# The last product of a packed-attention and gated-feed-forward kernel as one level of Strassen's seven products from batch 2 on

## The chip, the cores and the metric

The kernel runs on one core of one Trainium2 chip. A core has TensorE (in profiles PE for its matmuls and PEld for its weight loads), VectorE (DVE), ScalarE (ACT), GpSimd (POOL), and SyncE (SP), whose queue issues nearly all DMA transfers here. The metric is the device time of one execution in microseconds, the median of several runs.

## The reference

All inputs are float32. There are 8 batches, 8 heads, 576 tokens and a head width of 64; 32 packed queries stand for each head. The output has 4608 rows (8 × 576 tokens) of 512 columns.

```python
def sm_attn(qq, kk, vv):
    s = scale * np.matmul(qq, kk.transpose(0, 1, 3, 2))
    s = s - np.max(s, axis=-1, keepdims=True)
    a = np.exp(s)
    a = a / (np.sum(a, axis=-1, keepdims=True) + 1e-09)
    return np.matmul(a, vv)
p_packed = sm_attn(p, k, v)
x = sm_attn(q, p_packed, p_packed)      # then (B*S, 512)
h = x @ w_in                            # 512 -> 2048
g = h * (1.0 / (1.0 + np.exp(-1.702 * h)))
out = g @ w_out                         # 2048 -> 512
```

## The kernel before

**Two parts.** For each batch the attention makes a small matrix `a` (the softmax weights of the 576 tokens over 32 packed rows of 8 heads, 256 rows in all) and four chunks of a matrix `m` (the packed values times `w_in`, 256 × 2048). The feed-forward part then forms `h = m^T a`, passes it through the gate, and multiplies the result `g` by `w_out`. The matmuls of the feed-forward part work on float32 split in two: an upper part, rounded to the fp32r type (`mhi`, `ahi`, `ghi`, and part 0 of `wo`), and the rest, rounded likewise (`mlo`, `alo`, `glo`, part 1 of `wo`). A product of two such numbers is three matmuls: upper × upper, upper × lower, lower × upper.

**First product.** `h_mm` (L693 to L701) makes 128 of the 2048 hidden columns for one half of a batch, 288 tokens, in one bank of PSUM: 2 × 3 = 6 matmuls of 128 × 288 (L698). Two banks (`psh`) take turns.

**Gate.** ACT writes a tanh of `h` (`h_tanh`, L706), DVE multiplies it with `h` (`h_gate`, `h_over`, L688), ACT or DVE rounds the result to `ghi` (`h_upper`, L121 or L123), and DVE or POOL writes the rest to `glo` (`h_lower`, L685).

**Last product.** `out_mm` (L758, in `product`) adds, for one block of 128 hidden columns `f` and one block of 128 tokens `i`, three matmuls with the tokens' `g` as the stationary operand and 512 columns of `w_out` as the moving one to one of four PSUM banks `acc0` to `acc3`. A batch has four whole token blocks, so each `f` takes 12 matmuls of 512 columns. The last 64 tokens of each batch (`REST`) are put aside in SBUF (`over`), and two batches together make one more block of 128 tokens (`over_mm`). Over the whole kernel L758 stands for 1728 matmuls of 512 columns. After the last `f`, `out_take` copies a bank to SBUF and `store` writes 256 KB to the output.

**Attention of the next batch.** It runs among the feed-forward work of the current one. On PE it comes as blocks of small matmuls that use parts of the array: `scores1_mm` (L265), `pack` (L459), `scores2_mm` (L588) and `m_chunk` (L528, 8 matmuls for each quarter of `w_in`), and one small transposition (`pack_turn_mm`, L518). A float32 matmul that is not fp32r stands in the profile as two records. `w_in` stays in SBUF for the whole run. The loads of `k`, `v` and `q` of a batch have tiles from a pool with two buffers (`kqv`), so that `q` may be loaded while `v` is still being read.

**What sets the order.** A tuple `order` lists some 2,900 steps, and a loop at the end of the function calls them one after another; each engine runs its share in that order, and each DMA queue too. Semaphores between engines follow from the tiles that steps read and write.

Of the kernel before, what the change touches and what calls it, by code (L numbers as in the profile page):

```python
# [18 lines left out]


@with_exitstack
def kernel(
    ctx: ExitStack,
    tc: tile.TileContext,
    q: bass.AP,
# [7 lines left out]
):  # L33

    nc = tc.nc

    NFC, NP, P, FC = w_in.shape
    DM, DF = NP * P, NFC * FC
    D = P // 2
    B = q.shape[1]  # L60
    NH = q.shape[3] // NP
    S = 2 * NH
    KF = 2 * P
    NPK = pk.shape[2] // NP - KF
    G = S // NPK
    NF = DF // P
    CF = FC // P
    NB = S // P
    REST = S - NB * P
    KC = (S + P - 1) // P  # L70
    KLAST = S - (KC - 1) * P
    DEC = 3
    MB = 2
    LATE = [(B - 1, 2), (B - 1, 3)]
    SCALE = 1.0 / float(D) ** 0.5

    cst = ctx.enter_context(tc.tile_pool(name="cst", bufs=1))
    wk = ctx.enter_context(tc.tile_pool(name="wk", bufs=1))
    ps_acc = ctx.enter_context(tc.tile_pool(name="ps_acc", bufs=1, space=PSUM))
    ps_h = ctx.enter_context(tc.tile_pool(name="ps_h", bufs=2, space=PSUM))  # L80
    ps_b = ctx.enter_context(tc.tile_pool(name="ps_b", bufs=2, space=PSUM))

    ident = cst.tile([P, P], F32, name="ident")
    make_identity(nc, ident)

    minus = cst.tile([P, P], F32R, name="minus")
    nc.scalar.mul(minus, ident, -1.0)

    w_in_all = cst.tile([P, NFC, NP, FC], F32, name="w_in")
    w_in_sb = [w_in_all[:, i] for i in range(NFC)]  # L90
    w_in_end = w_in_all.rearrange("p c j f -> p (c j f)")[:, NFC * NP * FC - NP * S :]
    w_in_raw = w_in.bitcast(U16)
    w_out_raw = w_out.bitcast(U16)

# [21 lines left out]
    def bank_acc(i):
        return lambda name: ps_acc.tile([P, FC], F32, tag=f"acc{i}", name=name)
# [19 lines left out]


    def load(what, b, part):
        if (what, b) not in kq:  # L140

            if what == "q" and b == 0:
                t = w_in_end
            else:
                t = wk.tile([P, KC * DM], F32, tag="kqv", name=f"{what}_{b}", bufs=2)
            kq["t", what, b] = t
            if what == "k":
                kq["p", b] = t[:, : NP * NPK].rearrange("p (j n) -> p j n", n=NPK)
            if what == "v":
                kq[what, b] = t.rearrange("p (c e) -> p c e", e=DM)  # L150
            else:
                at = NP * NPK if what == "k" else 0
                t = t[:, at : at + NP * S]
                n = KF if what == "k" else NH
                kq[what, b] = [
                    i.rearrange("p (j s) -> p j s", j=NP) for i in (t[:, : NP * n], t[:, NP * n :])
                ]
        t = kq["t", what, b]
        if what == "v":
            main = (KC - 1) * DM  # L160
# [20 lines left out]
    raw = {}  # L181
    wo = {}
# [3 lines left out]


# [3 lines left out]
    def load_w(n, part=None):  # L191
        w = queue[n]
        i = slot_of(w)
# [4 lines left out]
        if not part:  # L198
            raw[i] = wk.tile([P, DM, 2], U32, tag=f"wo{i}", name=f"raw{i}")
        halves = raw[i].rearrange("p n w -> p (n w)").bitcast(U16)  # L200
# [3 lines left out]

    tops = wk.tile([P, 4, DM], U32, tag="late", name="tops")
    tops = [tops[:, i, :] for i in range(4)]
    for t in tops:
        nc.gpsimd.memset(t, 0)
    dec = {}
    top = {}

    def begin_w(n, part=None):
        top[n, part] = tops[(n + (part or 0)) % 4]  # L220
# [32 lines left out]

    def lower_w_copy(n, engine=nc.scalar):
        move(engine, wo[slot_of(queue[n])][:, 1, :], st["wl", n])

# [1301 lines left out]
```

## Time and profile before

| | us |
|---|---|
| median of 3 runs (691.46 to 691.87) | 691.49 |
| span of the profiled execution | 689.5 |
| PE busy (5020 matmul records) | 680.5 |
| DVE busy | 411.3 |
| ACT busy | 256.1 |
| POOL busy | 159.8 |

The span runs from the first to the last instruction of one profiled execution; the time of a run lies some 2 us above it. Matmuls are pipelined, and the recorded length of one is longer than the distance to the next; what a matmul costs is read from the starts of matmuls that follow each other without a wait.

### The profile page before, as it was taken

The numbers are of one execution on the slowest core, as the hardware profiler recorded it, in microseconds if no ns is written. First come the engines' busy times: TensorE is split into PE (matmuls) and PEld (weight loads), VectorE is DVE, ScalarE is ACT, GpSimd is POOL, SyncE is SP. The second block draws the span as 40 slices with busy tenths as digits, with TensorE's granted clock in tenths as the row PEclk, the third lists the DMA queues.
The fourth block names the chain that finished last, engine by engine and source line by source line (L and its number), as shares of the span: only waits on it lengthen the run. The fifth ranks groups of instructions, "written<-read, shape, count | busy, mean of one in ns | idle before, by whom it ended". The sixth has DMA issues, their size and how long they took to land.

```text
span 689.5 us, 13004 instructions
## 1 busy us (share of the span) xinstructions
PE 680.5 (99%) x5020; PEld 559.2 (81%) x5020; DVE 411.3 (60%) x1046; ACT 256.1 (37%) x617; POOL 159.8 (23%) x191
## 2 busy tenths in 40 slices
PE   8899999999999999999999999999999999999997
PEld 6678788888888888888778878888887878878885
DVE  5998877465565665546646458736565457664333
ACT  4886545222242234332324332523244322342220
POOL 2543351112520123221311012120221120310220
PEclk9999999999999999999999999999999999999999
DMA  9998602501135130430313420252301500010002
GB/s 343 397 355 247 252 37 50 177 16 35 62 90 137 39 111 4 104 120 1 92 54 87 138 61 1 82 130 73 115 17 62 130 1 1 16 62 1 1 1 77
DMA packets 55262, 65.20 MB, mean 95 GB/s; under 512 B 35808, under 2 KB 40864, under 8 KB 54176
## 3 DMA queue, kind: packets, MB, share of 16 engines
q1 hardware_dynamic: 55120, 64.23, 28.9%
q8 instruction: 40, 0.66, 0.4%
q14 instruction: 22, 0.18, 0.1%
q10 hardware_dynamic: 80, 0.13, 0.1%
HBM read 50.78 MB, written 13.57 MB: 93 GB/s over the span
## 4 chain that ended last, share of the span: by engine, by line
PE 96%; DVE 1%; ACT 1%; DMA 1%; POOL 0%; issue 0%; SPq 0%; DVEq 0%; ACTq 0%; POOLq 0%
PE acc L758 52%; PE h L698 30%; PE acc_over L758 6%; PE psm_None L528 4%; PE ps L588 1%; PE pspv L459 1%; PE ps L265 1%; DMA k<-k_last 1%; DVE w_in L234 0%; POOL x L623 0%; PE psm L528 0%; ACT tops L222 0%; ACT x L344 0%; PE pspt L518 0%; DVE x L599 0%
## 5 line engine op out<-in xcount | busy, mean ns | idle before, releaser
L758 PE MATMUL acc<-wo,ghi 128*128 128x512 f32 x1024 | 321.2, 395 | 0.0
L758 PEld LDWEIGHTS acc<-wo,ghi 128*128 128x128 f32 x1024 | 181.4, 188 | 34.8 <-issue 5.1
L706 ACT ACTIVATE g<-h 128x288 f32<-128x288 f32 x256 | 103.2, 411 | 273.8 <-PE h L698 246.8
L758 PE MATMUL acc<-wo,glo 128*128 128x512 f32 x512 | 201.6, 394 | 0.0
L685 POOL TENSOR_TENSOR glo<-g,ghi 128x288 fp32r<-128x288 f32 (+1 forms) x136 | 103.0, 765 | 425.2 <-ACT ghi L121 153.7
L688 DVE SCALAR_TENSOR_TENSOR g<-g,h 128x224 f32<-128x224 f32 (+1 forms) x256 | 105.1, 416 | 127.1 <-ACT g L706 126.1
L698 PE MATMUL h<-ahi,mhi 128*128 128x288 f32 x480 | 135.9, 298 | 0.1
L698 PE MATMUL h<-ahi,mlo 128*128 128x288 f32 x480 | 134.5, 295 | 0.3 <-DVE mlo L564 0.3
L758 PEld LDWEIGHTS acc<-wo,glo 128*128 128x128 f32 x512 | 96.1, 188 | 22.6 <-POOL glo L685 0.3
L698 PEld LDWEIGHTS h<-ahi,mhi 128*128 128x128 f32 x480 | 90.2, 188 | 20.0 <-DVE x L599 10.1
L698 PE MATMUL h<-alo,mhi 128*128 128x288 f32 x480 | 101.3, 292 | 0.0
L698 PEld LDWEIGHTS h<-ahi,mlo 128*128 128x128 f32 x480 | 90.4, 188 | 6.2 <-DVE mlo L564 0.5
L698 PEld LDWEIGHTS h<-alo,mhi 128*128 128x128 f32 x480 | 77.1, 188 | 0.1
L121 ACT CAST ghi<-g 128x224 fp32r<-128x224 f32 (+1 forms) x133 | 52.8, 404 | 50.5 <-DVE g L688 29.7
L685 DVE TENSOR_TENSOR glo<-g,ghi 128x288 fp32r<-128x288 f32 (+1 forms) x120 | 53.4, 447 | 20.5 <-ACT ghi L121 17.9
L688 DVE SCALAR_TENSOR_TENSOR over<-g,h 128x64 f32<-128x64 f32 x128 | 26.9, 215 | 36.0 <-ACT g L706 35.8
L123 DVE CAST ghi<-g 128x288 fp32r<-128x288 f32 (+1 forms) x123 | 37.9, 313 | 12.5 <-PE acc L758 9.5
L564 DVE TENSOR_TENSOR mlo<-psm_None,mhi 128x512 fp32r<-128x512 f32 x58 | 38.5, 677 | 2.6 <-ACT mhi L121 2.3
L758 PE MATMUL acc_over<-wo,ghi_over 128*128 128x512 f32 x128 | 39.8, 392 | 0.0
L528 PE MATMUL psm_None<-w_in,PT 64*32 64x512 f32 x496 | 33.0, 595 | 0.0
L758 PEld LDWEIGHTS acc_over<-wo,ghi_over 128*128 128x128 f32 x128 | 23.7, 188 | 4.8
L121 ACT CAST mhi<-psm_None 128x512 fp32r<-128x512 f32 x34 | 19.6, 585 | 21.0 <-PE psm_None L528 21.0
(108 smaller groups left out, 509.1 us busy)
## 6 DMA issues: line engine op xcount, KB each, us to landing
v<-v SPq DMA_DIRECT2D x8, 1024.0 KB, 5.4
o<-o SPq DMA_DIRECT2D x32, 256.0 KB, 3.2
raw<-w_out SPq DMA_DIRECT2D x16, 511.8 KB, 5.7
q<-q SPq DMA_DIRECT2D x14, 576.0 KB, 5.3
raw<-w_in SPq DMA_DIRECT2D x12, 511.8 KB, 7.7
k<-k_last SPq DMA_DIRECT2D x8, 640.0 KB, 4.7
k<-pk SPq DMA_DIRECT2D x8, 576.0 KB, 4.9
aside<-xb SPq DMA_DIRECT2D x56, 72.0 KB, 2.3
```

What stands on the lines that cost most here:

```text
L121: nc.scalar.copy(dst, src)
L123: engine.tensor_copy(dst, src)
L265: nc.tensor.matmul(bank[32 * j : 32 * j + 32, : k.shape[1]], kq["p", b][rows(eo), j, :], k, start=True, stop=True,)
L459: nc.tensor.matmul(bank[32 * j : 32 * j + 32, e * D : (e + 1) * D], aT[:, c, e, 32 * j : 32 * j + 32], vt[:, c, e0 : e0 + D], start=(c == ...
L528: nc.tensor.matmul(banks[eo][32 * j : 32 * j + 32, columns(part)], PT[rows(eo), j, :], w_in_sb[fc][rows(eo), j, columns(part)], start=True ...
L564: nc.vector.tensor_tensor(lo, bank[:, at], hi.bitcast(F32), op=ALU.subtract)
L588: nc.tensor.matmul(banks[eo][32 * j : 32 * j + 32, :NH], st["PT", b][rows(eo), j, :], kq["q", b][half][rows(eo), j, :], start=True, stop=True,
L685: engine.tensor_tensor(lo, src, hi.bitcast(F32), op=ALU.subtract)
L688: nc.vector.scalar_tensor_tensor(dst, th, 1.0, h, op0=ALU.add, op1=ALU.mult)
L698: nc.tensor.matmul(h[:, :NH], m[eo][part][:, fo : fo + P], a[:, eo * NH : (eo + 1) * NH], start=(n == 0), stop=(n == len(terms) - 1),)
L706: nc.scalar.activation(g, st["h", b, f, half][:, :NH], AF.Tanh, scale=1.702)
L758: nc.tensor.matmul(acc, gp[:, at : at + P], wo[f][:, part, :], start=(start and i == 0), stop=(stop and i == 2),)
```

## The change

Batch 0 keeps the last product of before. Everything behind it is rebuilt.

- A batch's tokens are cut into unequal halves of `NA` = 256 and `NB_` = 320. A round `n` is one half of a batch (`n` = 2 to 15, two for each batch from 1 on), or, twice, the 256 tokens that four batches put aside (`("over", 0)` and `("over", 1)`). Of the 320 tokens of an odd round, the first 64 are the ones put aside, now to a DRAM tensor (`over_kept`, by `hp_over`), and read back by `over_in`.
- A round has 8 pairs `p` of hidden blocks. For each pair `hp_mm` makes `h` of both blocks in a double bank `hh` (12 matmuls of 256 or 320 columns), and one tanh and one gate handle both. 
- A pair is then a 2 × 2 block product: two token blocks by two hidden blocks, times two hidden blocks by two column halves of `w_out` of 256. `sums_1` to `sums_3` make four sums of blocks of `g`; `g_upper` and `g_lower` round the seven blocks that are used. `product` does the seven products, each three matmuls of 256 columns, to seven half banks. `take_1` to `take_6` add these up when a round ends.
- The sums of blocks of `w_out` are made once, pair by pair (`conv_whole`, `conv_1` to `conv_4`, `conv_upper`, `conv_lower`) during rounds 2 to 5, and stay in SBUF (`RUNS`). Until a pair's sums are there, the pair is done in the way of before (`plain`): these are the 15 pairs of `PLAIN`; the other 113 of 128 use the seven products.
- Memory is laid out by hand in named regions. `w_in` is written to DRAM after batch 0 (`win_out`) and each quarter of it is read back for each later batch (`win_in`, 1 MB), since its place now holds the rounded `g` and some sums. For batches from 2 on `k`, `v` and `q` share one region, `KQ[0]`. Blocks of `g` before rounding have two places in turn (`g_words`), as have the rounded ones.

```diff
-    def product(acc, g, f, at, start, stop):
-        for i, (part, gp) in enumerate(((0, g[0]), (1, g[0]), (0, g[1]))):
-            nc.tensor.matmul(
-                acc, gp[:, at : at + P], wo[f][:, part, :],
-                start=(start and i == 0), stop=(stop and i == 2),
-            )
+    def hp_mm(n, p, j):
+        h_terms(hh()[:, j, :], n // 2, 2 * p + j, n % 2)
+    def hp_over(n, p):
+        b = n // 2
+        g = hp_view(n, p)[0][:, :, :REST]
+        dst = over_kept[b // 4][p].rearrange("p (j t) b r -> p j t b r", t=2)
+        nc.sync.dma_start(dst[:, :, b % 4 // 2, b % 2, :], g)
+    def over_in(n, p):
+        src = over_kept[n[1]][p].rearrange("p i b r -> p (i b r)")
+        nc.sync.dma_start(g_words(n, p, 0, 4 * P), src)
+    def sums_1(n, p, engine=nc.vector):
+        a, e = g_at(n, 1), g_at(n, 2)
+        src = g_words(n, p, a, 2 * (e - a)).rearrange("p (i t) -> p i t", i=2)[:, :, :P]
+        dst = g_raw(n, p, 4, 2).rearrange("p (i t) -> p i t", i=2)
+        by = g_raw(n, p, 0).unsqueeze(1).broadcast_to([P, 2, P])
+        engine.tensor_tensor(dst, src, by, op=ALU.subtract)
+    def sums_2(n, p, engine=nc.vector):
+        engine.tensor_tensor(g_raw(n, p, 6), g_raw(n, p, 5), g_raw(n, p, 1), op=ALU.add)
+    def sums_3(n, p, engine=nc.vector):
+        engine.tensor_tensor(g_raw(n, p, 7), g_raw(n, p, 3), g_raw(n, p, 6), op=ALU.subtract)
+    PRODUCT = {
+        1: (1, 0, 0), 6: (6, 0, 256), 5: (5, 1, 0), 7: (4, 1, 256), 2: (3, 2, 0), 3: (7, 2, 256),
+        4: (2, 3, 0),
+    }
+    def product(n, p, k):
+        block, i, at = PRODUCT[k]
+        hi, lo = (g_block(n, p, part, block) for part in range(2))
+        bhi, blo = moving(p, k)
+        add_up(n, i, at, 256, [(hi, bhi), (hi, blo), (lo, bhi)])
+    def take_3(n):
+        nc.vector.tensor_tensor(
+            o_words(n, 256, 512).rearrange("p (i t) -> p i t", i=2),
+            acc[1].rearrange("p (i t) -> p i t", i=2),
+            u2().unsqueeze(1).broadcast_to([P, 2, 256]), op=ALU.add,
+        )
+        at = KQ[b < 2 and what == "v"] if (what, b) != ("q", 0) else WIN + NFC * NP * FC - NP * S
...
-        (out_mm, 7, 14, 0), (out_mm, 7, 15, 0), (h_lower, 7, 14, 1), (h_gate, 7, 15, 1),
+        (hp_mm, 15, 1, 0), (g_upper, 15, 0, 0, act), (g_upper, 15, 0, 1, dve),
+        (g_lower, 15, 0, 1, dve), (hp_mm, 15, 1, 1), (g_lower, 15, 0, 0, dve), (product, 14, 7, 1),
```

The order of the instructions moves with it. On PE, in the middle of batch 4 before: `out_mm` (L758, hidden blocks of 128, `wo` and `ghi` or `glo` as operands) between the first products (L698) of single hidden blocks.

```order
L758 MATMUL acc_4_4407<-wo_584,ghi_2_4402 128x512 x2
L758 MATMUL acc_4_4407<-wo_584,glo_2_4403 128x512
L698 MATMUL h_0_5_4553<-ahi_0_4261,mhi_1_0_4416 128x288
L698 MATMUL h_0_5_4553<-ahi_0_4261,mlo_1_0_4417 128x288
L698 MATMUL h_0_5_4553<-ahi_0_4261,mhi_1_1_4355 128x288
L698 MATMUL h_0_5_4553<-ahi_0_4261,mlo_1_1_4356 128x288
L698 MATMUL h_0_5_4553<-alo_0_4262,mhi_1_0_4416 128x288
L698 MATMUL h_0_5_4553<-alo_0_4262,mhi_1_1_4355 128x288
L758 MATMUL acc_4_4442<-wo_584,ghi_2_4402 128x512 x2
L758 MATMUL acc_4_4442<-wo_584,glo_2_4403 128x512
```

And in the changed kernel, where the first half of a batch passes into the second (L698 is `h_terms`, L863 the matmuls of `product`; all rounded operands have names of regions).

```order
L698 MATMUL hh<-at_float32r 128x256 x12
L863 MATMUL acc_63<-at_float32r 128x256 x6
L863 MATMUL acc_64<-at_float32r 128x256 x6
L863 MATMUL acc_65<-at_float32r 128x256 x6
L863 MATMUL acc_66<-at_float32r 128x256 x3
L698 MATMUL hh<-at_float32r 128x320 x12
```

A stage of PE is now 12 matmuls of the first product and 21 matmuls of 256 columns, where two hidden blocks and 256 tokens took 12 of 512 columns.

DVE in the feed-forward work of a batch before (L688 gate and the part put aside, L123 rounding):

```order
L688 SCALAR_TENSOR_TENSOR g_0_12_3075<-g_0_12_3075,h_0_12_3058 128x288
L123 CAST ghi_12_3091<-g_0_12_3075 128x288
L688 SCALAR_TENSOR_TENSOR over_3_3096<-g_1_12_3094,h_1_12_3065 128x64
L688 SCALAR_TENSOR_TENSOR g_1_12_3094<-g_1_12_3094,h_1_12_3065 128x224
L123 CAST ghi_12_3091<-g_1_12_3094 128x224
```

DVE for one pair of an even round in the changed kernel (L691 is the gate, L826 to L834 the sums, L173 rounding, L841 `g_lower`):

```order
L841 TENSOR_TENSOR at_float32r<-at_float_349,at_float32r 128x512
L691 SCALAR_TENSOR_TENSOR at_float_349<-at_float_349,hh 128x512
L826 TENSOR_TENSOR at_float_349<-at_float_349 128x256
L830 TENSOR_TENSOR at_float_349<-at_float_349 128x128
L834 TENSOR_TENSOR at_float_349<-at_float_349 128x128
L173 CAST at_float32r<-at_float_349 128x384
L841 TENSOR_TENSOR at_float32r<-at_float_349,at_float32r 128x384
```

Three sums stand between a gate and the rounding now, and the two roundings of the rest are of 384 (448 in odd rounds) and 512 columns.

SP around the load of `q` in the middle of the run before (L447 brings the turned attention weights `aT` in, L171 loads `k` and `q`): `q` goes to a tile of its own.

```order
L447 DMA aT<-aside_4414 32x4x256 x2
L447 DMA aT<-aside_4414 32x256
L447 DMA aT<-aside_4414 32x4x256
L171 DMA q_4793<-q 128x1152 x2
L171 DMA k_4387<-k_last 128x1280
```

And in the changed kernel (L498 brings `aT` in, L814 is `hp_over`, L917 `keep`, L223 and L225 load `q`), with the semaphores that each waits for:

```order
L498 DMA at_float_92<-aside_2268 32x256 [waits DMAHW7_49]
L498 DMA at_float_92<-aside_2268 32x256
L814 DMA over_94<-at_float_349 256x1x64 [waits DMAHW1_49,DVE_49]
L223 DMA at_float_97<-q 128x1024 [waits DMAHW2_49,PE_49]
L225 DMA at_float_97<-q 128x1280 [waits DMAHW3_49,PE_49]
```

The load of `q` now waits for PE, that is for `pack`, which reads `v` in the same region. On PE, `pack` (L511) and the first use of that `q` (`scores2_mm`, L617) are one stage apart in a later batch of the changed kernel:

```order
L511 MATMUL b_68<-at_float_97,at_float_92 32x64 x4
L863 MATMUL acc_63<-at_float32r 128x256 x6
L562 MATMUL b_67<-at_float_74,at_float_243 128x128
L863 MATMUL acc_64<-at_float32r 128x256 x6
L863 MATMUL acc_65<-at_float32r 128x256 x6
L863 MATMUL acc_66<-at_float32r 128x256 x3
L698 MATMUL hh<-at_float32r 128x320 x6
L617 MATMUL b_67<-at_float_97,at_float_249 32x256
```

The blocks of small matmuls have moved too. Before, 14 of the `m_chunk` blocks follow a `scores2_mm`, 6 stand with both `scores1_mm` of a batch and 6 with a `pack`, with no large matmul between; with the 7 that stand otherwise there are 33 such blocks on PE behind the start. In the changed kernel 30 `m_chunk`, 13 `scores1`, 12 `scores2_mm` and 7 `pack` stand alone and 2 `m_chunk` with a `scores2_mm`: 64 blocks. 

## Rows read from the trace of the kernel before

**Rows 1.** The page's first part: the span, and busy time, share and count by engine, and from its second part the granted TensorE clock in 40 slices, in tenths.

```profile
span 689.5 us, 13004 instructions
PE 680.5 (99%) x5020; PEld 559.2 (81%) x5020; DVE 411.3 (60%) x1046; ACT 256.1 (37%) x617; POOL 159.8 (23%) x191
PEclk9999999999999999999999999999999999999999
```

**Rows 2.** The page's chain of waits that ended last, by engine and by line, as shares of the span.

```profile
PE 96%; DVE 1%; ACT 1%; DMA 1%; POOL 0%; issue 0%; SPq 0%; DVEq 0%; ACTq 0%; POOLq 0%
PE acc L758 52%; PE h L698 30%; PE acc_over L758 6%; PE psm_None L528 4%; PE ps L588 1%; PE pspv L459 1%; PE ps L265 1%; DMA k<-k_last 1%; DVE w_in L234 0%; POOL x L623 0%; PE psm L528 0%; ACT tops L222 0%; ACT x L344 0%; PE pspt L518 0%; DVE x L599 0%
```

**Rows 3.** The chain of waits in order of time: start, length and count of matmuls on it, for two runs of matmuls of 512 columns without another between.

```profile
666.57 7.53 PE acc L758 x33
674.10 11.01 PE acc_over L758 x48
```

**Rows 4.** The timeline of PE, start and length in us: the first matmuls of two neighbouring first products and the first matmul behind them. Twelve matmuls of 288 columns start from the first row to the second.

```profile
300.93 0.29 PE L698 MATMUL h<-ahi,mhi 128*128 128x288 f32 x1
...
302.51 0.63 PE L758 MATMUL acc<-wo,ghi 128*128 128x512 f32 x2
```

**Rows 5.** The timeline of PE and of its weight loads: matmuls of 128 columns with a new load each, back to back at the start.

```profile
14.67 2.72 PE L129 MATMUL warm<-ident 128*128 128x128 f32 x22
...
14.89 2.31 PEld L129 LDWEIGHTS warm<-ident 128*128 128x128 f32 x20
```

**Rows 6.** The timeline of PE around blocks of small matmuls: the block's start, and the start of the next large matmul. In the second stretch the last large matmul ahead, and in the first the second one behind, stand too.

```profile
24.85 0.77 PE L265 MATMUL ps<-k 64*32 64x320 f32 x16
25.55 0.40 PE L698 MATMUL h<-ahi,mhi 128*128 128x288 f32 x1
25.79 0.30 PE L698 MATMUL h<-ahi,mlo 128*128 128x288 f32 x1
...
50.87 0.40 PE L758 MATMUL acc<-wo,glo 128*128 128x512 f32 x1
51.20 1.09 PE L528 MATMUL psm_None<-w_in,PT 64*32 64x512 f32 x16
52.22 0.40 PE L698 MATMUL h<-ahi,mhi 128*128 128x288 f32 x1
...
69.74 1.32 PE L459 MATMUL pspv<-v,aT 128*32 128x64 f32 x80
71.00 0.73 PE L758 MATMUL acc<-wo,ghi 128*128 128x512 f32 x2
...
104.49 1.09 PE L528 MATMUL psm_None<-w_in,PT 64*32 64x512 f32 x16
106.48 0.73 PE L758 MATMUL acc<-wo,ghi 128*128 128x512 f32 x2
...
221.53 1.09 PE L528 MATMUL psm_None<-w_in,PT 64*32 64x512 f32 x16
223.80 0.73 PE L758 MATMUL acc<-wo,ghi 128*128 128x512 f32 x2
...
230.64 0.72 PE L588 MATMUL ps<-q,PT 64*32 64x288 f32 x16
231.15 1.06 PE L528 MATMUL psm_None<-w_in,PT 64*32 64x512 f32 x16
232.14 0.40 PE L698 MATMUL h<-ahi,mhi 128*128 128x288 f32 x1
```

**Rows 7.** Groups of DVE instructions by line and shape: count, busy us, mean ns of one, and idle time before them.

```profile
L688 DVE SCALAR_TENSOR_TENSOR g<-g,h 128x288 f32<-128x288 f32 x128 | 57.4, 450 | 80.9 <-ACT g L706 80.0
L688 DVE SCALAR_TENSOR_TENSOR g<-g,h 128x224 f32<-128x224 f32 x128 | 48.6, 382 | 46.3 <-ACT g L706 46.2
L564 DVE TENSOR_TENSOR mlo<-psm_None,mhi 128x512 fp32r<-128x512 f32 x58 | 38.5, 677 | 2.6 <-ACT mhi L121 2.3
L685 DVE TENSOR_TENSOR glo<-g,ghi 128x288 fp32r<-128x288 f32 x68 | 32.9, 487 | 10.5 <-ACT ghi L121 8.5 <-PE acc L758 0.3
L685 DVE TENSOR_TENSOR glo_over<-over,ghi_over 128x512 fp32r<-128x512 f32 x10 | 8.0, 797 | 3.1 <-ACT ghi_over L121 2.9
```

**Rows 8.** The tanh on ACT, likewise.

```profile
L706 ACT ACTIVATE g<-h 128x288 f32<-128x288 f32 x256 | 103.2, 411 | 273.8 <-PE h L698 246.8 <-POOL glo L685 15.3 <-DVE glo L685 7.8
```

**Rows 9.** DMA issues by kind: count, KB each, median us from issue to landing.

```profile
v<-v SPq DMA_DIRECT2D x8, 1024.0 KB, 5.4
o<-o SPq DMA_DIRECT2D x32, 256.0 KB, 3.2
q<-q SPq DMA_DIRECT2D x14, 576.0 KB, 5.3
aside<-xb SPq DMA_DIRECT2D x56, 72.0 KB, 2.3
aT<-aside SPq DMA_DIRECT2D x28, 128.0 KB, 2.6
```

**Rows 10.** The timeline of SP around one load of `q`, and of PE for that batch's `pack` and `scores2_mm`.

```profile
388.40 2.00 SPq L171 DMA_DIRECT2D q<-q  x2
...
387.02 1.32 PE L459 MATMUL pspv<-v,aT 128*32 128x64 f32 x80
...
399.46 0.72 PE L588 MATMUL ps<-q,PT 64*32 64x288 f32 x16
```

More of the change, by code (lines that the diff above doesn't have):

```diff
@@ L577, in m_again_copy @@
-    def m_again_copy(b, fc, eo, part=None, engine=nc.scalar):
-        at = columns(part)
-        move(engine, st["m", b, fc, eo][1][:, at], st["again", b, fc, eo, part][:, at])
-    def scores2_mm(b, half, banks=(bank_b, bank_b)):
-        st["x", 2, b, half] = x_tile(f"x2_{b}_{half}")
-        banks = [bank(f"ps2_{b}_{half}_{eo}") for eo, bank in enumerate(banks)]
+        hi, lo = (m_part(fc, eo, i)[:, at] for i in range(2))
+        t = st["bank", "m", b, fc, eo, part]
+        nc.vector.tensor_tensor(lo, t[:, at], hi.bitcast(F32), op=ALU.subtract)
@@ new lines, in take_4, with take_5, take_6, keep @@
+    def take_4(n):
+        nc.vector.tensor_tensor(
+            o_words(n, 768, 256), acc[1][:, 256:], o_words(n, 256, 256), op=ALU.add
+        )
+    def take_5(n):
+        o = o_words(n, 0, 512)
+        nc.vector.tensor_tensor(o, acc[2], o, op=ALU.add)
+    def take_6(n):
+        whole = any(not SET[m, p] for m, p in G_INDEX if m == n)
+        o = o_words(n, 512, 512 if whole else 256)
+        nc.vector.tensor_tensor(o, acc[3] if whole else acc[3][:, :256], o, op=ALU.add)
+    def keep(n, i, engine=nc.sync):
+        src = o_words(n, 0 if i else 512, 512)
+        at = n // 2 * S + (NB_ if n % 2 else 0) + i * P
+        engine.dma_start(out[at : at + P, :], src)
@@ new lines @@
+        (plain, 3, 4, 1, 1), (g_upper, 3, 6, 0, act), (sums_2, 3, 6, dve),
+        (conv_upper, 4, -1, dve), (sums_3, 3, 6, dve), (m_chunk, 2, 1, (6, 7), None),
+        (g_lower, 3, 6, 0, dve), (g_upper, 3, 6, 1, act), (hp_mm, 3, 7, 0),
+        (conv_lower, 4, -1, dve), (m_upper, 2, 1, 0, None, act), (win_in, 2, 2),
+        (m_upper, 2, 1, 1, None, dve), (g_lower, 3, 6, 1, pool), (hp_mm, 3, 7, 1),
+        (m_lower, 2, 1, 0), (m_lower, 2, 1, 1), (product, 3, 5, 1), (conv_whole, 3, 1, pool),
@@ new lines @@
+        (g_lower, 7, 5, 1, dve), (hp_tanh, 7, 6), (product, 7, 4, 6), (product, 7, 4, 5),
+        (hp_gate, 7, 6), (product, 7, 4, 7), (product, 7, 4, 2), (hp_over, 7, 6),
+        (sums_1, 7, 6, dve), (product, 7, 4, 3), (product, 7, 4, 4), (sums_2, 7, 6, dve),
+        (sums_3, 7, 6, dve), (m_chunk, 4, 1, (6, 7), None), (g_upper, 7, 6, 0, act),
+        (g_upper, 7, 6, 1, dve), (hp_mm, 7, 7, 0), (g_lower, 7, 6, 1, dve),
+        (m_upper, 4, 1, 1, None, act), (win_in, 4, 2), (g_lower, 7, 6, 0, dve),
@@ new lines @@
+        (product, 11, 4, 2), (hp_over, 11, 6), (sums_1, 11, 6, dve), (product, 11, 4, 3),
+        (product, 11, 4, 4), (sums_2, 11, 6, dve), (sums_3, 11, 6, dve),
+        (m_chunk, 6, 1, (6, 7), None), (g_upper, 11, 6, 0, act), (g_upper, 11, 6, 1, dve),
+        (hp_mm, 11, 7, 0), (g_lower, 11, 6, 1, dve), (m_upper, 6, 1, 0, None, act), (win_in, 6, 2),
+        (g_lower, 11, 6, 0, dve), (m_upper, 6, 1, 1, None, act), (hp_mm, 11, 7, 1),
+        (m_lower, 6, 1, 0), (product, 11, 5, 1), (hp_tanh, 11, 7), (m_lower, 6, 1, 1),
```

2458 lines of the change are left out of this document (1362 added, 1096 removed).

## The prediction

> **What bounds the kernel now.** [...] Then the chain of waits: 96% of it is PE, and 58% of the span is L758, the product that changes [rows 2]. So time follows the work on PE, and the other engines matter where they come near PE's time or are late for it. Recorded lengths of matmuls overlap, so starts are counted. Runs of 33 and of 48 matmuls of 512 columns last 7.53 and 11.01 us, 228 and 229 ns each [rows 3]; the chain's 58% over 1728 matmuls gives 231, and I take that, since it holds all of them [rows 2]. Twelve matmuls of 288 columns last from 300.93 to 302.51, 132 ns each [rows 4].
>
> **What a matmul of 256 columns costs.** None of full array size is in the trace. From the two points the slope is (231 - 132)/224 = 0.442 ns a column: 256 columns give 118 ns and 320 give 146. Below, 111 ns is conceivable (the slope of the fastest starts); above, 132, what 288 columns cost, bounds it, if something other than columns sets the distance. A weight load per matmul is such a thing: 22 matmuls of only 128 columns, each with a load, last 2.72 us, and 20 loads 2.31, about 112 ns apart [rows 5]. That is below 118, so I take 118. [...]
>
> **The product on PE.** Of 1728 matmuls of 512 columns 372 stay (192 in batch 0, 15 plain pairs of 12). The other 1356, 113 pairs of 12, become 113 x 21 = 2373 of 256 columns. Off: 1356 x 231 ns = 313.2 us. On: 2373 x 118 = 280.0. **Gain 33.2 us**, 294 ns a pair. The first product keeps its columns: 768 x (118 + 146) ns is what 1536 x 132 was, so 0.
>
> **Small matmuls on PE now stand alone.** A block costs its time inside and two edges. The row of 512 columns ahead of the block at 51.20 starts 0.33 us earlier in place of 0.23, an edge of 0.10; behind the block at 24.85 the next distance is 0.24 in place of 0.13, 0.11 [rows 6]. With 0.2 for edges a lone `m_chunk` costs 1.02 + 0.2, `scores1` 0.70 + 0.2, `pack` 1.26 + 0.2; with company 1.50 + 0.2 (`scores2_mm`), 2.27 + 0.2 (`pack`) and 1.99 + 0.2 (two `scores1`) [rows 6]. A lone `scores2_mm` is not in the trace behind the start: it is between its 0.51 ahead of `m_chunk` and the 0.70 of `scores1`, plus 0.2; I take 0.8. Before: 14 x 1.70 + 6 x 2.47 + 6 x 2.19 + 7 others of about 9.9 = 61.6 us. After: 30 x 1.22 + 13 x 0.90 + 12 x 0.80 + 2 x 1.70 + 7 x 1.46 = 71.5. **Loss 9.9 us.**
>
> **DVE.** Two-input instructions cost 487 ns for 288 columns and 677 for 512, the gate 382 for 224 and 450 for 288 [rows 7]: about 150 + 1.05 a column. Per pair of an even round DVE has a gate of 512 (688), sums of 256, 128 and 128 (419 + 2 x 284), `g_lower` of 512 and 384 (688 + 553), and one of two roundings (some 0.4): 3.3 us against 12 x 118 + 21 x 118 = 3.9 on PE; in odd rounds the gate is of 640 and one `g_lower` of 448, 3.5 against 12 x 146 + 2478 = 4.2. Over the kernel the counts of the new program times these lengths add up to some 185 us (sums +89, `g_lower` +68, adding up `take_*` +33, block sums of `w_out` +25, fewer and wider gates -35, rounding +5), so DVE rises from 411 to some 595 of 670, 89%. POOL and ACT change by less than 20 us. So PE stays ahead in nearly every stage, but with little room. The gate frees `hh` for the next first product: tanh of 640 (some 0.7, from 411 ns for 288 [rows 8]) and gate (0.82) take 1.6 of the 2.5 us of products that cover them; if DVE starts the gate over 0.9 us late, PE waits. The new waits of DVE upon itself (gate, three sums, rounding, each reading the last one's result) have behind them on DVE the attention's work; who waits is PE's next product, a stage later. I take 0.5 us for all of it, between 0 and rival B.
>
> **Transfers with PE behind them.** (1) `q` now waits for `pack`, in batches 2 to 7. Queued on SP behind it are only `hp_over` and `win_in`. From the end of `pack` to `scores2_mm` PE has 2.48 us of products, a transposition (0.15) and six matmuls of 320 (0.88): 3.5 us. The first half of `q` is 512 KB: between 3.2 us for 256 KB and 5.4 for 1 MB, about 4, plus 0.1 to issue [rows 9]. PE then stands 0.6 us, six times: **3.6 us**; at the 5.3 us of the old `q` 11, at 3.2 none. Before, 11 us lay between that load and its use [rows 10]. (2) The last of six `aT` loads, each some 0.45 us of SP apart, behind `keep` and so behind `take_6`, lands 2.6 us after its issue [rows 9]; `pack` stands one stage (4.2 us) behind the first. 0 to 1 us, six times; I take 0.25, nearer to nothing, since the first of the six may be issued before that stage begins: 1.5. (3) In the `over` rounds no first product covers anything: 256 KB in (3.2), sums and `g_lower` (1.7), then the place is free, some 5.1 us for two pairs against 4.96 on PE. 0 to 6 us for both rounds, I take 2. (4) `win_in` of 1 MB lands in 5.4 [rows 9] and has two stages (8 us) or more: 0, hidden by products; `hp_over` (64 KB, like `aside` with 2.3 us) has two stages until its place is written again: 0. Without that cover each would cost what it lacks. **Together 7.1 us.** Start and end keep their shape: 0.
>
> **Sum.** On the profiled execution 689.5 - 33.2 + 9.9 + 0.5 + 7.1 = 673.8; runs stand 2.0 above the span: **676 us.** The edges were counted in the 231 already to some part (clean runs are 229 [rows 3]); with 229 for the old matmuls and 117 for the new, the gain would be 1356 x 229 - 2373 x 117 = 32.9, so that does not move the sum.
>
> **Rivals.**
> A, PE alone decides: no wait of the last two parts shows, and 256 columns cost their fastest, 114. 691.5 - 33.2 - 2373 x 4 ns (9.5) + 9.9 = 659 (between that and the forecast lies the same mechanism with other sizes). For it: idle PE before is a few us [rows 1, 2]. Against: the two narrow places above.
> B, DVE becomes the bound from batch 2 on. The row of `glo_over` means 797 ns where the same shape from PSUM means 677 [rows 7]: DVE's two-input instructions are held up at times by something. With some 40 ns on 620 such instructions (25 us) and 33 ns for each of some 250 more waits on itself (8), DVE has 628 us, and with what it cannot use at the start and between tanh and gate (some 60) the run takes 688. It decides from about 4.0 us of DVE a stage. [...]
> C, slower: load and matmul do not overlap fully, and 256 columns cost as much as 288, 132 ns. Then 3141 matmuls of 256 (2373 and 768) cost 14 ns more, 44 us: 676 + 44 = 720. It decides from about 123 ns, where the gain is gone (16/3141 = 5 ns above 118). For it: the load's 112 ns is close. Against: twelve matmuls of 288 keep 132, which is 20 above the load's distance, without a sign of a floor.
> D, the seven products are not what runs: the counts of the new program (2373 of 256 columns) exclude it.
>
> **How the numbers follow.** Forecast (663 to 684) 0.70; A 0.12; B 0.10, about a third of it no better than now; C 0.08. Range 655 to 692: it leaves out C and a little of A. A measurement of this kernel tells 0.2% (1.4 us) from no change. Faster: 0.70 + 0.12 + 0.06 = 0.88; within 0.2%: 0.02; slower: 0.02 + 0.08 = 0.10.
>
> **What would show it.** In the new profile, starts of L863 in a row 118 ns apart (C: over 123); PE busy 97% or more (B: DVE near its whole span, and PE's idle time ended by DVE); idle time ahead of `scores2_mm` ended by the DMA of `q`, about 0.6 us six times; ahead of `pack` by `aT`; in the `over` rounds by DVE or DMA; blocks at 1.2 and 0.9 us. Wrong would be 118 in the first place: each ns of it is worth 3.1 us.

## The result and the profile after

The changed kernel takes 697.19 us (median of 4 runs, 696.11 to 697.79) where the kernel before takes 691.48 (691.25 to 691.87): a ratio of 1.0079, 95% interval 1.0065 to 1.0093. It is 5.7 us slower, where 676 and a gain were forecast, and lies outside the range of 655 to 692.

The first part of the page of the changed kernel (span, busy time by engine, then the granted clock in 40 slices), which answers to [rows 1]:

```profile
span 694.9 us, 15468 instructions
PE 671.4 (97%) x6037; PEld 594.4 (86%) x6037; DVE 594.0 (85%) x1204; ACT 309.5 (45%) x603; POOL 186.6 (27%) x202
PEclk9999999999999999999999999999999999999999
```

DVE's 594.0 us is the forecast 595 almost to the microsecond. PE is at 97%, not at 99%: it stands idle for some 23 us now, where it stood for 9. What it waits for, from the list of PE's waits (each row has the engine, line and tile that wait, what they wait for, the us in total, how many times, and the longest):

```profile
PE b L511 <- DMA at_float<-aside: 5.6, 5, 1.4
PE acc L863 <- POOL at_float32r L841: 1.9, 3, 0.8
PE hh L698 <- DVE at_float L691: 1.5, 3, 0.7
...
PE b L617 <- DMA at_float<-q: 0.2, 1, 0.2
```

The largest is `pack` (L511) waiting for `aT`; the wait for `q` that the prediction looked for is nearly absent. The timeline of PE in the last batch shows the price of a matmul and that wait, in brackets at the end of its row:

```profile
557.82 2.68 PE L863 MATMUL acc<-at_float32r 128*128 128x256 f32 x21
560.34 1.92 PE L698 MATMUL hh<-at_float32r 128*128 128x320 f32 x12
562.10 2.68 PE L863 MATMUL acc<-at_float32r 128*128 128x256 f32 x21
564.62 1.92 PE L698 MATMUL hh<-at_float32r 128*128 128x320 f32 x12
567.94 1.32 PE L511 MATMUL b<-at_float,at_float 128*32 128x64 f32 x80 [1.40 <-DMA at_float<-aside]
569.19 0.98 PE L863 MATMUL acc<-at_float32r 128*128 128x256 f32 x6
```

21 products of 256 columns start in 560.34 - 557.82 = 2.52 us, 120 ns each, and 12 of 320 in 1.76, 147 ns each [rows 3, 4 are the same reading before]. SP's queue at the same place:

```profile
562.07 0.83 SPq L917 DMA_DIRECT2D o<-at_float  x2
563.13 2.92 SPq L498 DMA_DIRECT2D at_float<-aside  x6
566.16 0.56 SPq L814 DMA_DIRECT2D over<-at_float  x1
568.64 0.36 SPq L223 DMA_DIRECT2D at_float<-q  x1
```

`keep` (L917), which stores finished output, waits for the last addition of the round before, and the six `aT` loads (L498) stand behind it; the last is issued by 563.13 + 2.92 = 566.05, and PE was ready for `pack` at 564.62 + 1.76 = 566.4. The load of `q` (L223) starts at 568.64, before `pack` ends: its first half overwrites only the first two of the five chunks of `v`, and those are read first.

The first over round holds the second cluster, from PE's timeline:

```profile
345.55 1.10 PE L863 MATMUL acc<-at_float32r 128*128 128x256 f32 x7 [0.43 <-POOL at_float32r L841]
347.20 0.50 PE L863 MATMUL acc<-at_float32r 128*128 128x256 f32 x2 [0.55 <-ACT at_float32r L171]
348.55 2.78 PE L863 MATMUL acc<-at_float32r 128*128 128x256 f32 x21 [0.85 <-POOL at_float32r L841]
351.94 0.73 PE L863 MATMUL acc<-at_float32r 128*128 128x256 f32 x4 [0.61 <-POOL at_float32r L841]
...
353.94 4.28 PE L863 MATMUL acc<-at_float32r 128*128 128x256 f32 x21 [0.38 <-DVE at_float32r L841]
```

Behind these waits, 21 matmuls last 4.28 us in place of 2.68: there the granted clock is 0.50 of full speed for 3.4 us (353.95 to 357.36), where it is 1.00 from 341.72 to 345.11 just before.

### The profile page after: what moved, and what is told of

Read it like the earlier page. It is cut to its first block, busy times and chain, and to the rows that moved or that the text cites. A ratio compares the mean times of both kernels' runs of the same rounds, so it can differ in the third digit from the quotient of the medians.

```text
span 694.9 us, 15468 instructions
## 1 busy us (share of the span) xinstructions
PE 671.4 (97%) x6037; PEld 594.4 (86%) x6037; DVE 594.0 (85%) x1204; ACT 309.5 (45%) x603; POOL 186.6 (27%) x202
## 5 line engine op out<-in xcount | busy, mean ns | idle before, releaser
L863 PE MATMUL acc<-at_float32r 128*128 128x256 f32 (+1 forms) x2553 | 349.3, 292 | 4.7 <-POOL at_float32r L841 1.9
L863 PEld LDWEIGHTS acc<-at_float32r 128*128 128x128 f32 x2553 | 327.5, 192 | 15.2 <-ACT at_float32r L171 2.7
L171 ACT CAST at_float32r<-at_float 128x512 fp32r<-128x512 f32 (+3 forms) x225 | 126.2, 569 | 202.5 <-PE acc L863 101.6
L698 PEld LDWEIGHTS hh<-at_float32r 128*128 128x128 f32 x1344 | 183.8, 189 | 35.0 <-DVE at_float L834 8.2
L698 PE MATMUL hh<-at_float32r 128*128 128x256 f32 (+1 forms) x1344 | 203.7, 300 | 1.6 <-DVE at_float L691 1.5
L841 DVE TENSOR_TENSOR at_float32r<-at_float,at_float32r 128x512 fp32r<-128x512 f32 (+3 forms) x192 | 130.4, 699 | 10.6 <-ACT at_float32r L171 6.6
L804 ACT ACTIVATE at_float<-hh 128x512 f32<-128x512 f32 (+1 forms) x112 | 72.9, 651 | 99.1 <-PE hh L698 93.0
L691 DVE SCALAR_TENSOR_TENSOR at_float<-at_float,hh 128x512 f32<-128x512 f32 (+1 forms) x112 | 83.8, 748 | 27.4 <-ACT at_float L804 27.1
L841 POOL TENSOR_TENSOR at_float32r<-at_float,at_float32r 128x512 fp32r<-128x512 f32 (+3 forms) x49 | 59.0, 1207 | 130.6 <-ACT at_float32r L171 46.9
L826 POOL TENSOR_TENSOR at_float<-at_float 128x256 f32<-128x256 f32 x30 | 22.2, 740 | 157.3 <-DVE at_float L691 154.8
L173 DVE CAST at_float32r<-at_float 128x512 fp32r<-128x512 f32 (+5 forms) x100 | 41.1, 411 | 19.9 <-PE acc L863 15.6
L826 DVE TENSOR_TENSOR at_float<-at_float 128x256 f32<-128x256 f32 x83 | 39.0, 470 | 2.4
L748 PEld LDWEIGHTS acc<-at_float32r 128*128 128x128 f32 x192 | 34.8, 188 | 7.0 <-issue 0.8
L830 DVE TENSOR_TENSOR at_float<-at_float 128x128 f32<-128x128 f32 x100 | 34.2, 342 | 4.7 <-POOL at_float L826 1.9
L171 ACT CAST at_float32r<-b 128x512 fp32r<-128x512 f32 (+1 forms) x55 | 29.8, 581 | 17.5 <-PE b L583 17.5
L698 PEld LDWEIGHTS h<-at_float32r 128*128 128x128 f32 x192 | 27.2, 189 | 7.7 <-DVE at_float L625 2.4
L698 PE MATMUL h<-at_float32r 128*128 128x256 f32 (+1 forms) x192 | 30.3, 301 | 1.3 <-DVE at_float L625 0.7
L834 DVE TENSOR_TENSOR at_float<-at_float 128x128 f32<-128x128 f32 x92 | 28.5, 310 | 2.1
```

The source lines that it names most:

```text
L171: nc.scalar.copy(dst, src)
L173: engine.tensor_copy(dst, src)
L691: nc.vector.scalar_tensor_tensor(dst, th, 1.0, h, op0=ALU.add, op1=ALU.mult)
L698: nc.tensor.matmul(t[:, : NH[half]], m_part(fc, eo, mp)[:, fo : fo + P], a_part(b, half, ap, eo), start=(n == 0), stop=(n == len(terms) - 1),)
L748: nc.tensor.matmul(acc[i], g0(f, gp)[:, i * P : (i + 1) * P], wo(f, wp), start=(start and n == 0), stop=(stop and n == 2),)
L804: nc.scalar.activation(g, h, AF.Tanh, scale=1.702)
```

## The experiments

The experiments that reorder the changed kernel do it just ahead of the loop that calls the steps, with one helper: `ahead(steps, of)` takes steps out of `order` and puts them in front of the step `of`.

### What narrow matmuls and lone blocks cost, in the kernel before

```diff
-            nc.tensor.matmul(
-                acc, gp[:, at : at + P], wo[f][:, part, :],
+            for c in range(0, DM, 256):
+                nc.tensor.matmul(
+                    acc[:, c : c + 256], gp[:, at : at + P], wo[f][:, part, c : c + 256],
```

> The kernel before with each of its 1728 matmuls of 512 columns made as two of 256 on the same stationary block. Price theory (a matmul has a fixed part of about 11 ns beside its columns, so 256 columns cost 120 where 512 cost 229): 1728 x 11 ns = 19 us more, 710. If 256 columns cost the 118 of the prediction and 512 the 231: 1728 x 5 = 9 us more, 700. If narrow matmuls were as dear as 288 columns (132): 60 us more, 752.

Measured: 706.84 us, ratio 1.0224 (1.0209 to 1.0240), 15.5 us more, or 9.0 ns for each of 1728 matmuls cut in two. Its PE timeline (L759 is the cut product):

```profile
300.58 0.64 PE L759 MATMUL acc<-wo,ghi 128*128 128x256 f32 x4
301.06 0.40 PE L759 MATMUL acc<-wo,glo 128*128 128x256 f32 x2
301.30 0.29 PE L698 MATMUL h<-ahi,mhi 128*128 128x288 f32 x1
```

Six in 0.72 us, 120 ns each, with nothing else changed and PE busy 99%. So 256 columns cost a little over half of 512 in this kernel as in the changed one; it is neither the 118 nor rival C's 132. The time lies between the two first theories, nearer to the first.

For the blocks, a large product was pulled between two neighbouring small blocks at 19 places:

```diff
+    for a in [s for s in order if s[0] in few and s[1] > 0]:
+        i = order.index(a)
...
+            if h[0] is out_mm and h not in used and i - j < 10:
...
+                    order.insert(i - 1, order.pop(j))
```

> The kernel before with a large product pulled between two neighbouring small blocks on PE: scores2_mm from m_chunk 13 times, m_chunk from pack 6 times, so 52 blocks where there were 33. If a lone block costs what the trace of the changed kernel shows (m_chunk 1.11 + 0.10, scores2_mm 0.74 + 0.10 against 1.70 for both; pack 1.35 + 0.19 and m_chunk 1.21 against 2.47): 13 x 0.36 + 6 x 0.28 = 6.4 us more, 698. If the edges of blocks are hidden by neighbours anyway: no change, 691.5.

Measured: 698.54 us, ratio 1.0103 (1.0086 to 1.0120), 6.9 us more. The first theory stands. A lone `m_chunk` there:

```profile
252.85 0.39 PE L758 MATMUL acc<-wo,glo 128*128 128x512 f32 x1
253.17 1.09 PE L528 MATMUL psm_None<-w_in,PT 64*32 64x512 f32 x16
254.19 0.40 PE L698 MATMUL h<-ahi,mhi 128*128 128x288 f32 x1
254.43 0.30 PE L698 MATMUL h<-ahi,mlo 128*128 128x288 f32 x1
```

From the last product to the first behind the block 1.34 us pass in place of 0.23, and the next distance is 0.24 in place of 0.13: 1.22 us for the block, the forecast figure.

### Is DVE the bound?

```diff
+    order = [s for s in order if s[0] not in (sums_1, sums_2, sums_3)]
```

> The changed kernel without its sums of blocks of g (sums_1 to sums_3 left out; the products read what stood in those places), which takes some 100 us of work and its chain from DVE. If PE bounds the changed kernel and waits cost it only at a few places: the waits of the over rounds and of the gate in rounds 2 to 5 go, 686 to 692, and the wait at pack stays. If DVE bounds it: 650 to 670, since DVE then has 490 us.

Measured: 689.68 us, ratio to before 0.9974 (0.9965 to 0.9984), 7.5 us below the changed kernel. Its page and its largest wait of PE:

```profile
PE 667.8 (97%) x6037; PEld 592.4 (86%) x6037; DVE 505.4 (73%) x929; ACT 306.2 (44%) x603; POOL 146.9 (21%) x138
```

```profile
PE b L511 <- DMA at_float<-aside: 6.1, 6, 1.6
```

89 us of DVE's work, and 40 of POOL's, gone brought 7.5 us. DVE's mean load is not the bound; it makes PE wait in places only, and the wait for `aT` stays without it.

### The wait for aT

```diff
+    for b in range(2, B):
+        n = 2 * b - 2
+        late = [s for s in order if s[:2] == (turn1_out, b) and order.index(s) > order.index((hp_over, n + 1, 0))]
+        ahead(late, (hp_over, n + 1, 0))
+        keeps = [i for i, s in enumerate(order) if s[:2] == (keep, n)]
+        ins = [s for s in order if s[:2] == (turn1_in, b)]
+        if order.index(ins[-1]) > keeps[0]:
+            ahead(ins, order[keeps[0]])
```

> The changed kernel with the aT loads ahead of keep on SP's queue, and the two late turn1_out of a batch ahead of hp_over. If queueing on SP makes PE wait at pack: 6 us less, 691. If the landing of the aside writes sets it: 2 to 3 us less, 694. If the wait is made up elsewhere: no change, 697.

Measured: 689.10 us, ratio to before 0.9973 (0.9961 to 0.9985): 8.1 us less than the changed kernel, more than any of the three theories gave, and faster than the kernel before. PE at the same place as above:

```profile
557.66 1.93 PE L698 MATMUL hh<-at_float32r 128*128 128x320 f32 x12
559.52 1.32 PE L511 MATMUL b<-at_float,at_float 128*32 128x64 f32 x80
```

`pack` follows the first product at once in all seven batches: 6.0 us of waits are gone, by starts. In this run's profiled execution the granted clock of the first over round (338 to 358 us) is 1.00, where it is 0.91 in the changed kernel: another 1.7. With the second half of that edit alone (the loads, `turn1_in`, ahead of `keep`; the writes, `turn1_out`, where they were):

> The changed kernel with the aT loads ahead of keep on SP's queue and nothing else moved. If the queue place behind keep (and so behind take_6) is the whole cause of the wait at pack: 689, as with turn1_out moved too. If the landing of the last aside write is the larger part: 693 to 695.

Measured: 695.15 us (692.60 to 697.03), ratio 1.0051 (1.0029 to 1.0074). PE's waits for transfers there:

```profile
PE b L617 <- DMA at_float<-q: 3.6, 4, 1.3
...
PE b L511 <- DMA at_float<-aside: 1.9, 2, 1.6
```

So the place behind `keep` was two thirds of the wait for `aT`; most of the rest is one wait of 1.6 us, whose loads stood behind the landing of the writes. And a wait for `q` appears. Its 3.6 us in all are the forecast's figure by luck: four waits of up to 1.3 us where six of 0.6 were forecast. The time from issue to landing of `q`'s first half (smallest, median, largest), in the changed kernel, in this one, and in the one before it with both halves of the edit:

```profile
DMA to landing us min/median/max: 3.4/4.1/8.3
```

```profile
DMA to landing us min/median/max: 3.6/5.0/8.3
```

```profile
DMA to landing us min/median/max: 3.5/4.0/8.4
```

`keep` writes 512 KB ahead of `q` in the last two alike, and the landing is longer in one of them only. So these writes do not explain the 0.9 us by themselves; what does stays open.

### The first over round

Three edits, each for one suspect. DVE's load: the attention's work goes to round 8.

```diff
+    o = ("over", 0)
+    ahead([(m_lower, 4, 2, 0), (m_lower, 4, 2, 1)], (product, o, 7, 1))
+    ahead([(sum2, 4, 1)], (product, 8, 0, 3))
...
+    ahead([(a_upper, 4, 1, None, act), (a_lower, 4, 1, dve)], (product, 8, 2, 1))
```

POOL's slow `g_lower` (L841 of 384 columns takes 1033 ns on average on POOL and 592 on DVE in the changed kernel), in the kernel with the early `aT` loads:

```diff
+    order = [
+        (*s[:-1], dve) if s[0] is g_lower and s[1] == ("over", 0) and s[2] < 4 else s for s in order
+    ]
```

The two places for the blocks read back, in the kernel with the early `aT` loads: a third place, and each `over_in` one place earlier.

```diff
     def g_words(n, p, at, m):
+        if n == ("over", 0):
+            return words((DEC, DEC + G_RAW, AT)[p % 3] + at, m)
...
+        order.insert(order.index(s), (over_in, o, p))
```

> The changed kernel with the attention's work for the second half of batch 4 (sum2, norm2, turn2, a_upper, a_lower) moved from the first over round to round 8, and m_lower to the end of the over round. If DVE and POOL are too full there: 4 to 6 us less (waits of 4.2 us and the stretch at half clock of 1.7), 691 to 693. If the landing of over_in sets it: no change, 697.

> The changed kernel with the early aT loads and the g_lower steps of pairs 0 to 3 of the first over round on DVE in place of POOL. If POOL's length of g_lower (1.0 to 1.3 us against 0.55 to 0.68) and the instructions of DVE that are held up beside it make PE wait there: 2 to 3 us less than the early loads alone, 686 to 687. If DVE is full there: no change or slower, 689 to 690.

> The changed kernel with the early aT loads and, in the first over round, a third place for the blocks read back (the aT region, which is free there), with each over_in one place earlier. If the chain of load, sums, rounding and reuse of two places makes PE wait there (3.0 us of waits in the run with the early loads): 2 to 3 us less than that run, 686 to 687. If DVE and POOL are too slow there whatever lies ready: 689.

Measured: 697.36 us (ratio 1.0089, 1.0071 to 1.0106), 689.75 (0.9973, 0.9963 to 0.9983) and 692.68 (1.0016, 1.0007 to 1.0026). None gains on its base (697.19 for the first, 689.10 for the others). The first two give the time of their theory of no gain; the third is 3.6 us slower than its base, which neither of its theories has. The busy times of the stretch from 338 to 358 us (length, then PE, PEld, DVE, ACT, POOL with counts, granted clock, DMA share, GB/s), in the changed kernel and with the attention's work away:

```profile
338.00:358.00 20.00, 16.78 (x123) 14.59 (x122) 18.22 (x36) 7.64 (x14) 8.20 (x9) 0.91 0.57 191
```

```profile
338.00:358.00 20.00, 16.79 (x130) 15.00 (x129) 11.79 (x29) 6.53 (x13) 7.59 (x8) 0.91 0.56 195
```

DVE is busy 18.2 of 20 us there. Relieved of 6.4 us, it leaves PE no better off, and the trace of that run says what PE then waits for. DVE (the first sum), ACT (the rounding) and, behind ACT, PE, each with its wait in brackets:

```profile
349.24 0.42 DVE L826 TENSOR_TENSOR at_float<-at_float 128x256 f32<-128x256 f32 x1 [4.13 <-DMA at_float<-over]
```

```profile
349.32 0.51 ACT L171 CAST at_float32r<-at_float 128x384 fp32r<-128x384 f32 x1 [3.49 <-DMA at_float<-over]
```

```profile
349.88 0.50 PE L863 MATMUL acc<-at_float32r 128*128 128x256 f32 x2 [1.20 <-ACT at_float32r L171]
```

They wait for a block that is read back. SP's queue with that load (`over_in`, L818, in the third row), and the time to landing of all 16 such loads of the run (smallest, median, largest):

```profile
338.88 0.33 SPq L818 DMA_DIRECT2D at_float<-over  x1
339.98 0.33 SPq L297 DMA_DIRECT2D at_float<-w_kept  x1
340.48 0.32 SPq L818 DMA_DIRECT2D at_float<-over  x1
```

```profile
DMA to landing us min/median/max: 2.4/2.6/8.7
```

The load took 8.7 us. It stands behind 1 MB of `w_kept` (`win_in`); that this makes it slow was not tried. In the changed kernel the largest is 7.2. So with DVE relieved the transfers set most of the round, as in the second theory of that run: of PE's waits in it, 3.9 us by starts, the 2.9 from that row on lie behind landings. The third place does not refute them: ACT's waits for blocks read back fall there from 5.5 us in its base to 2.3, but DVE still has the attention's work in its order, ACT's waits for DVE's last sum grow from 4.5 to 7.7, and PE's waits in the round grow, by starts, from 3.0 to 4.7. (A wait for `q` of 1.4 us came back as well.) So each of these two edits takes away one cause and leaves the other, and no run takes away both. With `g_lower` on DVE POOL is busy 2.7 us of the stretch, DVE 18.6, and PE's waits stay at 2.9. The next run takes the attention's work off DVE and `g_lower` off POOL together, with the early `aT` loads and the gate moved as below; the transfers stay as they are:

> The changed kernel with the early aT loads, the gate ahead, and in the first over round both moves that failed alone: the attention's work for the second half of batch 4 in round 8, and g_lower of pairs 0 to 3 on DVE. If either engine alone keeps PE waiting there (DVE busy 18.6 of 20 us with g_lower on it, POOL late without): the waits of the over round fall from 3 us to under 1. If all of that is saved: 685 to 686; if round 8 pays it back in waits for the gate, as in the run that only moved the attention: 688 to 690.

Measured: 689.17 us, ratio 0.9968 (0.9958 to 0.9979). The same stretch:

```profile
338.00:358.00 20.00, 19.11 (x148) 17.86 (x147) 15.97 (x39) 7.69 (x14) 2.10 (x3) 1.00 0.51 177
```

PE is at 19.1 of 20, where it was at 17.7 with the early loads alone; its named waits there fall to 0.6 us, and by starts from 3.0 to 1.8. The time does not fall: in round 8 the gate (L691) now stands on DVE behind the next batch's attention (L480 turns it), and PE behind the gate. DVE first, then PE:

```profile
385.13 0.78 DVE L480 STREAM_TRANSPOSE at_float<-at_float 128x576 f32<-128x576 f32 x1
385.84 0.65 DVE L691 SCALAR_TENSOR_TENSOR at_float<-at_float,hh 128x512 f32<-128x512 f32 x1
```

```profile
386.54 1.70 PE L698 MATMUL hh<-at_float32r 128*128 128x256 f32 x12 [1.26 <-DVE at_float L691]
```

A nearly full DVE alone did not make PE wait here. In the stretch just behind the over round of the same run DVE is busy 20.85 of 22 us, and PE all 22:

```profile
358.00:380.00 22.00, 22.00 (x201) 19.84 (x207) 20.85 (x40) 8.64 (x16) 5.28 (x7) 1.00 0.24 73
```

### The gate, the load of q, and all together

All three have the early `aT` loads. The gate ahead of other work on DVE:

```diff
+    ahead([(hp_gate, 4, 1)], (m_lower, 2, 2, 0))
+    ahead([(m_lower, 2, 2, 0)], (keep, 3, 0))
+    ahead([(hp_gate, 4, 7)], (g_lower, 4, 6, 1, dve))
+    ahead([(m_lower, 3, 0, 1), (turn2, 3, 0)], (product, 5, 3, 3))
```

The same, and `scores2_mm` later:

```diff
+    for b in range(2, B):
+        turn = next(s for s in order if s[:3] == (scores2_turn, b, 0))
+        ahead([s for s in order if s[:3] == (scores2_mm, b, 0)], turn)
```

The third has these and the third place as well.

> The changed kernel with the early aT loads and, at three places of rounds 4 and 5, the gate ahead of attention work or g_lower on DVE. If the waits of PE for the gate (0.8, 0.8 and 1.1 us) come only from the order on DVE: 2 to 3 us less than the early loads alone, 686 to 687. If DVE is full there, so that the wait goes to a later product: 689.

> The changed kernel with the early aT loads, the gate ahead at three places, and the first scores2_mm of batches 2 to 7 half a first product (0.9 us) later on PE. If the waits at scores2_mm in the run with the gate ahead (2.2 us, two times) are the load of q that waits for pack: they are gone, 686 to 687. If the attention behind scores2_mm has no slack: the waits come back at m_chunk or in later first products, 689 or more.

> The changed kernel with all four moves (early aT loads, gate ahead, late scores2_mm, third place). If the waits found are separate: 697.2 - 8 - 2 - 2 - 3, about 682, and no stretch at the lower clock in the first over round. If they only pass on to the next wait: 687 to 689.

Measured: 688.75 us (0.9961, 0.9948 to 0.9973), 690.06 (0.9980, 0.9971 to 0.9990) and 690.54 (0.9986, 0.9977 to 0.9996). The gate's waits, 2.3 us, are gone from the list of PE's waits, and only 0.35 us of the median with them, which is within the spread of these runs. In the profiled execution a wait for `q` stands in their place:

```profile
PE b L617 <- DMA at_float<-q: 2.2, 2, 1.2
```

That the one follows from the other is not shown. SP issues the same loads and stores around `q` in the same order in both runs, and the profiled execution took 690.25 us, 1.5 above the median of its seven; it also has a stretch of the over round where 27 matmuls last 5.21 us (27 last 3.39 at the clock of 1.00 in the changed kernel), and a mean granted clock of 0.996, where the profiled execution with the early loads alone has 0.998, and 1.00 in that round.

With `scores2_mm` later that wait is gone, and the gate of the next pair is late instead, at four batches alike:

```profile
321.93 1.29 PE L698 MATMUL hh<-at_float32r 128*128 128x320 f32 x7 [0.32 <-DVE at_float L691]
```

The last run is above even the 687 to 689 of its second theory. Past the early `aT` loads no move gains more than 0.35 us, alone or with others. That a saved wait is taken by the next one is plain where `scores2_mm` is later (four batches alike) and in round 8; elsewhere it fits the traces and is not shown. The fastest version is 688.75, 0.4% faster than the kernel before.

## Why the prediction was wrong, step by step

The sum was right in its form, too large in the gain and too small in most of the terms that stand against it. Each term, in us, by the starts of matmuls in the profiled execution of the changed kernel; a distance between large matmuls counts as a wait where it is over 0.13 us too long, and as an edge where it is about 0.10:

| term | forecast | measured | how |
|---|---|---|---|
| product | -33.2 | -28.3 | 1356 x 230.5 before, 2373 x 119.8 after (means without waits and edges) |
| first product | 0 | +2.8 | 768 x (119.6 + 146.6) for 1536 x 131.3 |
| small blocks and edges | +9.9 | +13.1 | blocks 57.1 to 65.3, edges 4.8 to 9.7 |
| `aT` | +1.5 | +6.0 | `pack` late in five batches |
| `q` | +3.6 | +0.3 | |
| over rounds | +2 | +7.1 | 4.2 of waits and 1.7 of the clock at 0.50 in the first, 1.2 in the second |
| DVE, rounds 2 to 5 | +0.5 | +3.3 | gate and `take_*` late |
| end | 0 | +1.8 | last matmul 6.7 us from the end, 4.8 before |
| together | -15.7 | +6.1 | the span moved by +5.4 |

**The step that failed by most is that of the waits,** 7.6 us in the forecast and 18.5 measured with the end: 7.1 in the over rounds and 6.0 for `aT` are the most of it. Of these the wait for `aT` is shown to be a matter of the queue: with the six loads and two of the writes ahead of `keep` and `hp_over` it is gone, and the kernel is faster than before. The prediction had found the place ("behind `keep` and so behind `take_6`") and the landing time of 2.6 us, and then took 0.25 of its 0 to 1, where five waits of 0.7 to 1.5 us came. It gave the loads a stage of 4.2 us, counted from where they stand in the order, not from their queue: the first is issued when `keep` is through, the six issues take 2.9 us and the landing some 2 more, and `pack` was due 3.3 us behind the first of them (566.4 against 563.13).

**The price of a narrow matmul,** "the slope is (231 - 132)/224", failed too. The two ends held some edges behind small blocks, as the prediction suspected of the 231; but a line through the clean 131.3 and 230.5 still gives 117.1 at 256 columns, and 119.8 was measured. The widths do not lie on one line: 288 columns, at 131.3, are 1.8 below the middle of 256 and 320 (133.1). So halves of 256 and 320 cost more than two of 288, which the straight line put at 0 and the table has at 2.8. The cut matmuls give the price by itself: two of 256 cost 9.0 ns more than one of 512. Some 5.5 of the 7.7 us lost in the first two rows are the 1.6 to 1.8 ns above 118 on 3141 matmuls. The right order of the queue alone leaves the kernel just faster than before, as the run with it shows (689.10); the forecast price alone would have done so too by an estimate (697.2 - 7.7 = 689.5) that takes in no new waits.

**The load of `q`** was priced right (4.1 us to the landing against the 4 of the forecast, whose further 0.1 us to issue was an estimate that no row shows) but its start was not: it need not wait for the end of `pack`.

**The over rounds** were the place named, with the transfer mis-sized: 3.2 us were taken for 256 KB, and one such load took 7.2 in the changed kernel, 8.7 with DVE relieved. The attention's work on DVE, which the prediction did not count there, is the second cause: with it in place an earlier load did not help. Which share each has stays open. At the end, put at 0, four stores are issued one behind the other by SP, from 689.75 on for 2.43 us, where before SP and ACT issued one each in 0.56.

**The small blocks** were right: 1.22 us for a lone `m_chunk`, and 19 blocks set apart in the kernel before cost 6.9 us. Of the 3.2 us by which their row is above the forecast some 2 are edges of 0.10 us that stand behind a wait of PE, not behind a block. **DVE's sum** was right as well (594.0 for 595, though `sums_1` to `sums_3` took 102 in it for 89 and other terms less), and so was that PE stays ahead of it on the whole: rival B is refuted by the run without sums as the bound of the kernel, and holds in stretches. Rival C is refuted (119.8, and 123 decides), and so is A (119.8 in place of 114, and waits). No rival ended at 697: the case that was missing is a dearer matmul and several waits, each small, together.

## What to carry to other kernels

Take the price of a smaller matmul from a cut of the old one, or at least from clean distances: halving the columns cost 9 ns for each cut matmul here, 4% of its time, where seven products for eight save 12.5%. Where an algorithm takes work off the bounding engine and gives it to a second one that goes to 85%, that engine's busy share does not tell where PE will wait: at 95% of 22 us it cost nothing here, at 91% of 20 us it went with 4 us of waits. Look at the stages with the least cover, here the rounds without a first product, and count all that stands between a load and its matmul there, the landing beside other transfers included. Where removing one suspect gains nothing, remove it together with the next before clearing it. In a queue shared by loads and stores, ask for each moved load which store stands ahead of it and what that store waits for: moving two kinds of steps in that queue was worth 8 us here and turned the sign.

## What the runs showed of the hardware that was not expected

DVE's small sums took longer where an instruction of POOL ran beside them. In the changed kernel 92 sums of 128 columns (L830) that no POOL instruction overlaps take 290 ns each on average, and 8 that one overlaps 940. One of them, with POOL's instruction beside it:

```profile
344.56 1.07 DVE L830 TENSOR_TENSOR at_float<-at_float 128x128 f32<-128x128 f32 x1 [0.75 <-POOL at_float L826]
```

```profile
344.49 1.00 POOL L841 TENSOR_TENSOR at_float32r<-at_float,at_float32r 128x384 fp32r<-128x384 f32 x1
```

The DVE instruction ends at 345.63 and POOL's at 345.49, 0.14 us earlier. In seven of the eight POOL began first, and each of these seven sums ends 0.15 us behind POOL's instruction; in the eighth DVE began first, and it took 283 ns. What makes them longer was not tried. Over the kernel DVE's time is still 594.0 us, against 595 forecast without it, and not the 628 of rival B, though these sums mean 342 ns and so are 52 longer, more than the 40 that B asked of each.

In the changed kernel a load began while a matmul block still read the later chunks of what stood in its place: the load of `q` waits only for the matmuls that read the two chunks that its first half overwrites. In the last batch it began at 568.64, 0.55 us before the first matmul behind `pack` (569.19), against the 0.6 us of the forecast wait.
